# A linear-attention layer and its two-matrix MLP on one core: the four small products of an attention group are gathered into common stretches of TensorE, whose places follow a count of instructions

## Chip, core and metric

The kernel runs on one core of a Trainium2 chip. The time is that of one execution in microseconds on the device; lower is better. The kernel before was timed in three runs: 470.63, 470.05 and 470.16 us, median 470.16. One further execution was profiled, and all rows below are from it: its span, from the first to the last instruction, is 470.0 us.

## What is computed

For each of 4 batches and 8 heads a 48x48 state is carried over 768 steps: decayed by a gate, increased by an outer product, read by a query. The result, 3072 tokens of 384, goes through two matrices with a clipped square between them.

```python
    f = 1.0 / (1.0 + np.exp(-f_logit))
    for t in range(S):
        state = f[:, :, t, :, None] * state + np.einsum('bhd,bhe->bhde', k[:, :, t], v[:, :, t])
        y[:, :, t] = np.einsum('bhd,bhde->bhe', q[:, :, t], state)
...
    h = x @ w_in
    g = np.where(pos, h, np.where(neg, 0.0, (h + beta) ** 2 / (4.0 * beta)))
    return (g @ w_out).astype(np.float32)
```

## The kernel before

**The MLP.** Tokens are taken in 6 steps of 128 positions (4 batches, so 512 columns). A step has 16 units, one for each 128 of the 2048 hidden features: 96 units, numbered 0 to 95. `unit_1` computes a hidden block with 9 matmuls of 128x512 (`mm_in`, L265): inputs and weights are split into a high and a low part, and three of the four products are kept, for 3 slices of the input. ScalarE and VectorE then apply the activation and split it again (L268 to L282); `unit_2` adds its part of the output with 9 more matmuls (`mm_out`, L289). TensorE runs `unit_1` of unit u and then `unit_2` of unit u-1.

**The attention.** A step has 4 pairs of heads; two pairs form a group. The groups of steps 1 to 5 are named by their first pair: 4, 6, 8, ... 22. A group needs on TensorE: *scores* (`scores_of_two`, L657: keys times queries, masked afterwards on VectorE at L663), *states* (`states_by_parts`, L791, from keys that were transposed before: on TensorE, L676, for step 1, on VectorE, L690, from step 2 on), and *outputs* in three parts: `begin` and the last part (`attended`, L712: masked scores times values) and between them the products of queries and carried states (L739). The result is rounded into `x` (L695, L696), and part of it is moved between partitions by six DMAs (`moved`, line L307). All these are small float32 matmuls of 48 to 64 rows.

**The order.** `Plan` collects all operations with a cost from `COST`, deduces a start time for each, and the program is written in that order. TensorE's own order is that of the calls: at unit u after `unit_1(u)` come the visits that two tables list. `TURNS` gives for a pair the unit of its transposition, `VISITS` for a group the units of scores, of `begin` together with states, and of outputs. A run of small products between two large ones is called a *stretch* here. Where the plan sees TensorE idle for over 500 ns, it fills the gap with products of zeros (`warm`, L342).

**Loads.** Weights, keys and queries, gates and values come over SP's queue in the order of the plan.

Of the kernel before, what the change touches and what calls it, by code (L numbers as in the profile page):

```python
# [23 lines left out]
C = 128  # L24
# [25 lines left out]
SMALL_PRODUCTS = ("scores", "scores_half", "heads", "thirds", "both", "begin", "before", "part", "states", "parts", "turn")  # L50
# [3 lines left out]
COST = dict(mm=227, narrow=120, scores=1000, scores_half=500, heads=960, thirds=1020, both=1090, begin=480, before=930, part=560, states=850, parts=830, turn=350, first=110, last=95,  # L54
# [3 lines left out]

LOOK, MARGIN, GAP = ("ACT", "DVE"), 100, 3000

TURNS = {4: 6, 5: 6, 6: 9, 7: 9, 8: 16, 9: 16, 10: 23, 11: 23, 12: 28, 13: 28, 14: 35, 15: 35, 16: 43, 17: 43, 18: 53, 19: 53, 20: 58, 21: 58, 22: 69, 23: 69}
VISITS = {4: (6, 7, 8), 6: (9, 11, 12), 8: (16, 20, 23), 10: (23, 25, 28), 12: (28, 32, 35), 14: (35, 41, 43), 16: (43, 47, 53), 18: (53, 56, 58), 20: (58, 64, 69), 22: (69, 73, 74)}
# [3 lines left out]
AFTER = {0: (('turn', 0), ('turn', 1)), 1: (('states', 0),), 3: (('turn', 2), ('turn', 3)), 4: (('states', 2),)}  # L66

# [15 lines left out]
class Plan:  # L83
# [7 lines left out]
    def add(self, engine, cost, emit, *deps, kb=0, near=0):  # L91
# [24 lines left out]

    def order(self):
        index = {o: n for n, o in enumerate(self.ops)}
        for o in reversed(self.ops):
            tail = o.cost + (LANDING + PER_KB * o.kb + (ADDING if o.engine == "POOL" else 0) if o.kb else o.near)  # L120
            o.late = min((u.late - o.lag(u) for u in o.users), default=0) - tail - o.early
# [12 lines left out]
        while done < len(self.ops):  # L134
# [28 lines left out]
            o.start = t  # L163
            free[e] = t + o.cost
# [17 lines left out]
def gla_moe(ctx: ExitStack, tc: tile.TileContext, ff, kqd, f0, vv, vad, vbd, wd, fixedd, gates, values, headsd, out):  # L182
# [22 lines left out]
    state, ds = sd[:R, 0:NP * B * D].rearrange("r (g e) -> r g e", e=D), sd[:R, NP * B * D:]  # L205
# [4 lines left out]
    later = y3[:, 0, 0:2 * B * D].bitcast(F32)  # L210
# [10 lines left out]
    f0s = const.tile([128, NI * NT * B + 1], F32, name="f0s")  # L221
    half, up, down, top_of = (const.tile([128, 1], F32, name=a) for a in ("half", "up", "down", "top_of"))
# [105 lines left out]
    set_ds = add("POOL", 200, lambda: fresh(ds[:, 2 * B * D:]))  # L328
# [16 lines left out]
    add("PE", 4000, lambda: warm(12), set_zeros)  # L345
# [176 lines left out]
    def elementwise(n):  # L522
# [10 lines left out]
        elif i == 0:  # L533
            c["lv"] = dma(va if p == 0 else vb, vad if p == 0 else vbd, 512 if p == 0 else 768)
        else:
            c["lv"] = dma(v[k], vv[i, p // 2], 384, old(n - 4, "y", "st"), att[2]["st"], moved[1] if i > 1 else None)
# [12 lines left out]
        if i > 0:  # L549
# [3 lines left out]
            def decayed():  # L553
                for b in range(B):
                    nc.scalar.activation(ds[:, at + b * D:at + (b + 1) * D], state[:, p * B + b], AF.Copy, scale=whole(kq[p])[:R, b:b + 1])  # L555

            c["db"].append(sca(B * COST["decay"], decayed, d, state_of[i - 1, p // 2], old(n - 2, "y", "se"), set_ds))
# [80 lines left out]
    def borrowed(k):  # L638

        return [(6, ph[(k + 1) % 2].rearrange("p (b c) -> p b c", b=B), [gs[k - 1]["3"]]), bank(2)]  # L640
# [6 lines left out]
    def scores_of_two(n, k):  # L647
# [13 lines left out]
        c["am"] = d["am"] = []  # L661
        for h, (b, ps, _) in enumerate(held):
            o = vec("dve", lambda h=h, ps=ps: nc.vector.tensor_tensor(  # L663
                out=masked(n)[h], in0=by_block(ps), in1=mask_t.rearrange("u (o t) -> u o t", o=1).broadcast_to([C, 2 * B, T]), op=ALU.mult),
                c["sc"], ready["mask_t"], old(n - 4, "y"), att[2]["y"], att[2]["st"])
            c["am"].append(o)
        freed(k, held, *c["am"])
# [32 lines left out]
    def attended(n, other):  # L700
# [4 lines left out]
        def emit():  # L705
            for m in range(B):
                for e, k in TILES:
# [5 lines left out]
                                     masked(n)[h][half, block], start=other and m == 0, stop=not other and m == B - 1)  # L713
# [3 lines left out]
    def begin(n):  # L717
# [6 lines left out]
        c["yb"] = add("PE", "begin", attended(n, True), c["am"], c["lv"], d["lv"], [b[2] for b in held])  # L724

    def outputs(n):
# [5 lines left out]
        def emit():  # L732
            for k, before in ((1, later), (0, ds)):
                for m in range(B):
                    for e, h in TILES:
# [4 lines left out]
                                         start=False, stop=False)  # L740
# [6 lines left out]
        def third(t):  # L747
            return [moved.get(i - 1)] + c["se"] if t == NT else [free]
# [29 lines left out]
    def states_by_parts(n, k):  # L778
# [3 lines left out]
        held = borrowed(k)  # L782
        sums = [wide(b[1])[:R, 0:2 * B * D] for b in held]

        def emit():
            for e in range(2):
# [6 lines left out]
        c["st"] = d["st"] = add("PE", "parts", emit, c["kn"], d["kn"], c["lv"], d["lv"], [b[2] for b in held])  # L793
        s = state[:, p * B:(p + 2) * B].rearrange("r b e -> r (b e)")
        o = vec("sums", lambda: nc.vector.tensor_tensor(out=later, in0=sums[0], in1=ds[:, 0:2 * B * D], op=ALU.add),
                c["st"], c["db"], d["db"], old(n - 2, "y", "se"), moved.get(i - 1))
# [7 lines left out]
        freed(k, held, o, z)  # L804
# [196 lines left out]

    for n, u in TURNS.items():
        groups.setdefault(u, []).append((1, n))
    for n, at in VISITS.items():
        for kind, u in zip((2, 3, 0), at):
            groups.setdefault(u, []).append((kind, n))
    for u in range(len(order_of)):
# [3 lines left out]
        for kind, n in sorted(groups.get(u, [])):  # L1011
            if kind == 0:
                outputs(n)
            elif kind == 1:
# [5 lines left out]
            elif kind == 2:  # L1020
                scores_of_two(n, u)
            else:
                begin(n)
                states_by_parts(n, u)
# [13 lines left out]
    with tc.manual_schedule():  # L1038
        idle, loaded = 0, False
        for o in plan.order():  # L1040
# [3 lines left out]
            if o.engine == "PE":  # L1044
# [148 lines left out]
```

## Time and profile before

| | |
|---|---|
| median of 3 runs | 470.16 us (470.05 to 470.63) |
| span of the profiled execution | 470.0 us |
| TensorE busy (matmuls) | 464.1 us, 99% |
| VectorE busy | 368.7 us, 78% |
| ScalarE busy | 264.9 us, 56% |
| granted clock of TensorE | full in all 40 slices |
| DMA | 54.34 MB, mean 116 GB/s |

Busy time of TensorE is the union of pipelined matmuls, with modelled ends; a matmul's own duration (390 ns) is longer than its place in the stream. So the useful measure is the distance between the starts of two groups of matmuls.

### The profile page before, as it was taken

Reading aid. Unit: us, or ns where it says so; the run is one execution under the profiler, and the core shown is the slowest. Engines: PE = TensorE matmul, PEld = TensorE weight load, DVE = VectorE, ACT = ScalarE, POOL = GpSimd, SP = SyncE. Lnnn points to the kernel's source line nnn. Section 1 sums busy time; section 2 is a strip of 40 time slices with the busy share of each in tenths; the row PEclk is TensorE's granted clock in tenths of the full one; section 3 lists DMA queues with packets and bytes.
Section 4 is the critical chain, followed back from the end, with each engine's and each line's share of the span. In section 5 each row is a group of like instructions: output and inputs, shape, how many; then the busy total and the mean of one; then the engine's idle time right before and its main releaser. Section 6 shows DMA issues by size and latency. Waiting matters only on the chain.

```text
span 470.0 us, 10963 instructions
## 1 busy us (share of the span) xinstructions
PE 464.1 (99%) x4551; PEld 378.1 (80%) x4551; DVE 368.7 (78%) x704; ACT 264.9 (56%) x483; POOL 25.5 (5%) x67
## 2 busy tenths in 40 slices
PE   9999999999999999999999999999999999999996
PEld 4887888778888888888888888888888888888885
DVE  7989998998999988999889879665766565655553
ACT  4589888955464654645545465544455444544443
POOL 4100020020000001002000002000000000000000
PEclk9999999999999999999999999999999999999999
DMA  8788758363031241401133141133403233423211
GB/s 295 244 269 275 257 170 269 131 176 107 1 81 78 63 120 70 135 23 47 49 90 94 52 138 57 56 81 100 158 20 113 74 101 89 158 89 91 89 45 70
DMA packets 21331, 54.34 MB, mean 116 GB/s; under 512 B 3328, under 2 KB 5504, under 8 KB 21280
## 3 DMA queue, kind: packets, MB, share of 16 engines
q1 hardware_dynamic: 21184, 53.53, 36.3%
q8 instruction: 36, 0.59, 0.5%
q14 instruction: 15, 0.12, 0.1%
q10 hardware_dynamic: 96, 0.10, 0.1%
HBM read 44.76 MB, written 4.72 MB: 105 GB/s over the span
## 4 chain that ended last, share of the span: by engine, by line
PE 81%; DMA 9%; DVE 6%; ACT 2%; issue 1%; SPq 0%; ACTq 0%; DVEq 0%
PE po L289 38%; PE ph L265 37%; DMA raw<-in_w 8%; PE pa L739 2%; PE pa L712 2%; DVE bits L397 2%; DVE w_lo L402 1%; PE ph L657 1%; DMA kq<-in_kq 1%; ACT bits L395 1%; DVE x L696 1%; PE pa L791 1%; DVE glo L282 1%; PE ph L791 1%; DVE act L276 1%
## 5 line engine op out<-in xcount | busy, mean ns | idle before, releaser
L265 PE MATMUL ph<-x,w_hi 128*128 128x512 f32 x570 | 145.3, 390 | 0.4 <-ACT w_hi L401 0.3
L268 ACT ACTIVATE act<-ph,half 128x512 f32<-128x512 f32 x96 | 65.9, 687 | 116.2 <-PE ph L265 115.3
L265 PEld LDWEIGHTS ph<-x,w_hi 128*128 128x128 f32 x570 | 106.7, 188 | 23.6 <-ACT w_hi L401 0.7
L276 DVE SCALAR_TENSOR_TENSOR act<-ph,act 128x512 f32<-128x512 f32 x96 | 66.1, 688 | 53.2 <-ACT act L271 52.1
L279 ACT CAST ghi<-act 128x512 fp32r<-128x512 f32 x96 | 59.6, 620 | 58.4 <-DVE act L276 58.1
L289 PE MATMUL po<-ghi,w_hi 128*128 128x512 f32 x287 | 85.7, 400 | 0.1
L289 PE MATMUL po<-ghi,w_lo 128*128 128x512 f32 x287 | 82.8, 390 | 0.0
L289 PE MATMUL po<-glo,w_hi 128*128 128x512 f32 x287 | 82.6, 389 | 0.0
L282 DVE TENSOR_TENSOR glo<-act,ghi 128x512 fp32r<-128x512 f32 x96 | 66.1, 689 | 18.2 <-ACT ghi L279 16.3
L265 PE MATMUL ph<-x,w_lo 128*128 128x512 f32 x285 | 80.0, 389 | 0.0
L690 DVE STREAM_TRANSPOSE kn<-kq 32x128 f32<-32x128 f32 x224 | 67.8, 302 | 3.6
L289 PEld LDWEIGHTS po<-ghi,w_lo 128*128 128x128 f32 x287 | 53.9, 188 | 11.5
L289 PEld LDWEIGHTS po<-glo,w_hi 128*128 128x128 f32 x287 | 53.9, 188 | 11.5
L265 PEld LDWEIGHTS ph<-x,w_lo 128*128 128x128 f32 x285 | 53.5, 188 | 11.1
L271 ACT ACTIVATE act<-act 128x512 f32<-128x512 f32 x96 | 60.7, 632 | 2.8
L289 PEld LDWEIGHTS po<-ghi,w_hi 128*128 128x128 f32 x287 | 52.0, 188 | 11.6 <-ACT ghi L279 0.7
L414 DVE TENSOR_REDUCE ok<-raw 128x1 f32<-128x512 f32 x48 | 31.2, 679 | 6.2 <-DMA raw<-in_w 6.0
L491 POOL COPY end<-w 128x4 f32<-128x4 f32 (+1 forms) x20 | 8.4, 419 | 259.9 <-DVE w L487 259.6
L487 DVE TENSOR_TENSOR_SCAN w<-f,least_w 128x512 f32<-128x512 f32 (+1 forms) x18 | 20.8, 1158 | 2.2 <-ACT f L483 2.2
L395 ACT ACTIVATE bits<-raw,top_of 128x512 uint32<-128x512 fp8e4 (+1 forms) x25 | 18.4, 741 | 6.7 <-DMA raw<-in_w 6.7
L494 DVE TENSOR_TENSOR_SCAN f<-f,rec 128x512 f32<-128x512 f32 (+1 forms) x18 | 20.8, 1157 | 0.1
L555 ACT ACTIVATE sd<-sd,kq 112x48 f32<-112x48 f32 x80 | 19.5, 326 | 1.1 <-POOL kq L504 1.1
(120 smaller groups left out, 382.6 us busy)
## 6 DMA issues: line engine op xcount, KB each, us to landing
raw<-in_w SPq DMA_DIRECT2D x21, 511.6 KB, 4.7
kq<-in_kq SPq DMA_DIRECT2D x18, 512.0 KB, 4.9
raw<-in_w SPq DMA_DIRECT2D x18, 512.0 KB, 3.6
out_y<-raw SPq DMA_DIRECT2D x17, 256.0 KB, 2.1
f<-in_f SPq DMA_DIRECT2D x16, 256.5 KB, 3.0
v<-in_v SPq DMA_DIRECT2D x10, 384.0 KB, 4.8
raw<-in_w SPq DMA_DIRECT2D x12, 256.0 KB, 2.9
kq<-kq SPq DMA_DIRECT2D x30, 64.2 KB, 2.7
```

The lines of the kernel that those rows point to most:

```text
L265: nc.tensor.matmul(ps[:, to], w_in(w_hi if high else w_lo, j, kt), xt[:, kt, t, c], start=(n == 0), stop=(n == 8))
L268: nc.scalar.activation(a, ps, AF.Relu, bias=half, scale=0.5)
L271: nc.scalar.activation(a, a, AF.Square)
L276: nc.vector.scalar_tensor_tensor(out=a, in0=ps, scalar=1.0, in1=a, op0=ALU.max, op1=ALU.min)
L279: nc.scalar.copy(hi, a)
L282: nc.vector.tensor_tensor(out=lo, in0=a, in1=hi.bitcast(F32), op=ALU.subtract)
L289: nc.tensor.matmul(po[e][:, c], w_out(part, j, e), g[:, of], start=(j == 0 and n == 0 and c.start == 0), stop=(j == NJ - 1 and n == 2))
L395: m = sca(COST["bits"] * n // W, lambda: nc.scalar.activation(t, top, AF.Abs, bias=top_of, scale=2.0 ** 30), loaded, made[k - 4] if k >= 4 ...
L414: seen.append(vec("dve", lambda z=z, op=op: nc.vector.tensor_reduce(out=ok[:, 1 + NG + z + c:2 + NG + z + c], in_=words_of(raw[2])[1].bitc ...
L487: s1 = vec(COST["scan"] if count == 1 else 602, lambda bwd=bwd, u0=u0, u1=u1: nc.vector.tensor_tensor_scan(out=wide(w[:, u0:u1]), data0=bw ...
L494: s2 = vec(COST["scan"] if count == 1 else 602, lambda fwd=fwd, b0=b0, b1=b1: nc.vector.tensor_tensor_scan(out=fwd, data0=fwd, data1=wide( ...
L690: nc.vector.transpose(kn[n % 2][u:u + 32, ::-1, r:r + 32], src[:, :, u:u + 32])
```

## The change

The four products of a group get their own unit each: `VISITS` has four entries, for scores, states, `begin` and outputs, and entries of different groups fall on the same unit, so that their products form one stretch. `visit` writes them in the order begin, states (if the scores of the group were earlier), scores, outputs, states (if the scores are in the same visit). `TURNS` lists a group once, and both its pairs are transposed there.

Buffers: the decayed states get a second buffer (`ds` in turn), the sum of state and decay gets its own (`later`, before a part of `y3`), states take banks 0 and 1 of PSUM when no outputs are under way, and where scores and states share a visit, ScalarE copies one half of the scores out of PSUM before it is masked. After `begin`, ScalarE copies 8 values of its result (`seen_y`), and the outputs wait for that copy.

The plan gets a model of the loading of TensorE's instructions: `fetched` counts instructions, takes blocks of 256 of which the first ends at 185, and delays an operation if the block it enters was asked for less than 4300 ns ago. Zeros are now decided inside the plan (`zeros_for`) and count as instructions.  The scratch of dynamic DMA is cut to 4096.

```diff
+INSTRUCTIONS = dict(scores=32, scores_half=16, heads=32, thirds=32, both=128, begin=64, before=128, part=64, states=64, parts=128, parts_last=64, zeros=24, turn=8)
+BLOCK, FIRST_BLOCK, AHEAD, FETCH = 256, 185, 40, 4300
...
-VISITS = {4: (6, 7, 8), 6: (9, 11, 12), 8: (16, 20, 23), 10: (23, 25, 28), 12: (28, 32, 35), 14: (35, 41, 43), 16: (43, 47, 53), 18: (53, 56, 58), 20: (58, 64, 69), 22: (69, 73, 74)}
+TURNS = {4: 4, 6: 7, 8: 11, 10: 20, 12: 25, 14: 35, 16: 40, 18: 52, 20: 58, 22: 66}
+VISITS = {4: (5, 5, 8, 8), 6: (8, 10, 10, 13), 8: (20, 20, 22, 22), 10: (22, 25, 28, 28), 12: (28, 33, 33, 40), 14: (40, 40, 43, 43), 16: (43, 48, 55, 55), 18: (55, 56, 56, 61), 20: (61, 61, 73, 73), 22: (73, 74, 74, 77)}
...
+def zeros_for(o, idle):
+    gap = o.start - idle if idle else 0
...
+    return int(gap * 0.9 / 230) if gap > 500 else 0
...
         o = Op(engine, cost, emit, flat, kb, near)
+        if engine == "PE":
+            o.count = INSTRUCTIONS.get(kind) or 2 * max(1, round(cost / (COST["mm"] if cost % COST["mm"] == 0 else COST["narrow"])))
...
+    def fetched(self, o, zeros):
+
+        self.at += 2 * zeros
+        t, step, last = o.start, o.cost / o.count, self.at
+        end = self.at + o.count
+        marks = sorted([(b - AHEAD, 0, b) for b in self.blocks(last + AHEAD, end + AHEAD)] + [(b, 1, b) for b in self.blocks(last, end)])
+        for at, kind, b in marks:
+            t += (at - last) * step
+            last = at
+            if kind:
+                t = max(t, self.came.get(b, 0))
+            else:
+                self.came[b + BLOCK] = t + FETCH
+        self.at = end
+        return t + (end - last) * step - o.start
...
-            c["db"].append(sca(B * COST["decay"], decayed, d, state_of[i - 1, p // 2], old(n - 2, "y", "se"), set_ds))
+            c["db"].append(sca(B * COST["decay"], decayed, d, state_of[i - 1, p // 2], old(n - 4, "y", "se"), set_ds))
...
+            if h == 1 and copied:
+                need = sca("copy", lambda ps=ps: nc.scalar.copy(masked(n)[1], by_block(ps)), need, past)
+                source = masked(n)[1]
...
-        c["yb"] = add("PE", "begin", attended(n, True), c["am"], c["lv"], d["lv"], [b[2] for b in held])
+        o = add("PE", "begin", attended(n, True), c["am"], c["lv"], d["lv"], [b[2] for b in held])
+        c["yb"] = sca("small", lambda: nc.scalar.copy(seen_y.rearrange("u (b c) -> u b c", b=B), held[0][1][0:1, :, T - 1:T + 1]), o)
...
+    def visit(u):
+
+        new, made, begun, ended = ([n for n, at in VISITS.items() if at[k] == u] for k in range(4))
+        held = [n for n, at in VISITS.items() if at[2] <= u <= at[3]]
+        for n in begun:
+            begin(n)
+        for n in made:
+            if n not in new:
+                states_by_parts(n, u, False)
+        for n in new:
+            scores_of_two(n, u, n in made)
+        for n in ended:
+            outputs(n)
+        for n in new:
+            if n in made:
+                states_by_parts(n, u, not held)
```

Three places show what moves. **TensorE at unit 4**, early in the program: the last large products of `unit_1(4)`, the state products of step 0 (L770) and the first large product of `unit_2(3)`. Before:

```order
L265 MATMUL ph_110<-x_85,w_hi 128x512 x6
L265 MATMUL ph_110<-x_85,w_lo 128x512 x3
L770 MATMUL pa_107<-v,am_78 48x48 x8
L770 MATMUL pa_107<-v,am_79 48x48 x8
L289 MATMUL po_112<-ghi_89,w_hi 128x512
L289 MATMUL po_113<-ghi_89,w_hi 128x512
```

After, from the third product of zeros that stands behind the same state products (L818 here) to the same large product:

```order
L382 LDWEIGHTS zeros
L382 MATMUL po_117<-zeros 128x512
L723 MATMUL pa_110<-fixed,kq_68 128x112 x4
L382 LDWEIGHTS zeros
L382 MATMUL po_117<-zeros 128x512
L382 LDWEIGHTS zeros
L382 MATMUL po_117<-zeros 128x512
L382 LDWEIGHTS zeros
L382 MATMUL po_117<-zeros 128x512
L723 MATMUL pa_111<-fixed,kq_69 128x112 x4
L329 MATMUL po_115<-ghi_89,w_hi 128x512
```

The transpositions of pairs 4 and 5 (L723; `kq_68` and `kq_69` hold their keys) have come here from unit 6, and three products of zeros stand ahead of each.

**TensorE at units 35 to 41**, the middle of the program. Before, the outputs of group 12 (L712 is their end) are followed by the scores of group 14 (L657) at unit 35:

```order
L712 MATMUL pa_108<-am_77,v 48x64
L712 MATMUL pa_107<-am_76,v 48x64
L712 MATMUL pa_108<-am_77,v 48x64
L657 MATMUL ph_110<-kq_70 64x64
L657 MATMUL pa_109<-kq_70 64x64
L657 MATMUL ph_110<-kq_70 64x64
```

and the states of group 14 (L791) come at unit 41, behind its `begin`:

```order
L712 MATMUL pa_107<-am_78,v 48x64
L712 MATMUL pa_108<-am_79,v 48x64
L712 MATMUL pa_107<-am_78,v 48x64
L791 MATMUL pa_109<-v,kn_80 48x48
L791 MATMUL ph_110<-v,kn_80 48x48 x2
L791 MATMUL pa_109<-v,kn_80 48x48 x2
```

After, all stand at unit 40: the scores of group 14 (L697), the outputs of group 12 (L787, then L759) and the states of group 14 (L839). The first join:

```order
L697 MATMUL pa_112<-kq_71 64x64
L697 MATMUL ph_114<-kq_71 64x64
L697 MATMUL pa_112<-kq_71 64x64
L787 MATMUL pa_110<-kq_68,later 48x64
L787 MATMUL pa_111<-kq_69,later 48x64
L787 MATMUL pa_110<-kq_69,later 48x64
```

and the last:

```order
L759 MATMUL pa_111<-am_77,v 48x64
L759 MATMUL pa_110<-am_76,v 48x64
L759 MATMUL pa_111<-am_77,v 48x64
L839 MATMUL pa_112<-v,kn_80 48x48
L839 MATMUL ph_114<-v,kn_80 48x48 x2
L839 MATMUL pa_112<-v,kn_80 48x48 x2
L839 MATMUL ph_114<-v,kn_80 48x48 x2
```

No large product is left between the four; the stretch has 448 instructions where the longest before has 320.

**ScalarE at unit 22**: the activation of unit 21 ends and that of unit 22 begins.

```order
L311 ACTIVATE act_84<-act_84 128x512
L319 CAST ghi_89<-act_84 128x512
L308 ACTIVATE act_83<-ph_113,half 128x512
L772 COPY seen_y<-pa_110 1x8
L311 ACTIVATE act_83<-act_83 128x512
L595 ACTIVATE ds<-sd,kq_71 112x48 x4
L523 ACTIVATE f_67<-f_67 128x513
```

The copy `seen_y` stands between the two steps of the activation of unit 22 (L308 and L311); before nothing stood there.

## Rows read from the trace of the kernel before

**Rows 1.** The page: the span, the busy time of TensorE (PE matmuls, PEld weight loads), and the granted clock in 40 slices, in tenths.

```profile
span 470.0 us, 10963 instructions
PE 464.1 (99%) x4551; PEld 378.1 (80%) x4551; DVE 368.7 (78%) x704; ACT 264.9 (56%) x483; POOL 25.5 (5%) x67
PEclk9999999999999999999999999999999999999999
```

**Rows 2.** All that TensorE's matmuls waited for: us in total, times, longest us.

```profile
PE ph L342 <- DVE zeros L315: 1.1, 1, 1.1
PE ph L265 <- ACT w_hi L401: 0.3, 1, 0.3
```

**Rows 3.** The chain of work that ended last, around three stretches: start us, us, what. First scores alone, then outputs and scores joined, then outputs alone; large products stand on both sides.

```profile
103.42 2.04 PE ph L265 x9
106.55 2.27 PE po L289 x9
...
159.48 2.04 PE ph L265 x9
161.52 1.04 PE pa L739 x64
163.94 2.27 PE po L289 x9
...
372.32 2.04 PE ph L265 x9
374.36 1.04 PE pa L739 x64
375.85 2.27 PE po L289 x9
```

**Rows 4.** TensorE's products of the scores by form, from the list of lines: count, then busy us and mean ns of one. The ten groups share them.

```profile
L657 PE MATMUL pa<-kq 48*64 48x64 f32 x320 | 11.3, 219 | 0.0
L657 PE MATMUL ph<-kq 48*64 48x64 f32 x320 | 11.3, 219 | 0.0
```

**Rows 5.** TensorE in order of time at unit 4: start us, us, operation, count.

```profile
41.67 1.43 PE L265 MATMUL ph<-x,w_hi 128*128 128x512 f32 x5 [0.26 <-ACT w_hi L401]
...
43.72 0.93 PE L770 MATMUL pa<-v,am 128*48 128x48 f32 x32
44.57 0.96 PE L289 MATMUL po<-ghi,w_hi 128*128 128x512 f32 x3
```

**Rows 6.** VectorE in order of time: the second scan of pair 4's gates, and the keys (L497) and queries (L499) of pairs 4 and 5; the rows between are left out.

```profile
35.54 1.22 DVE L494 TENSOR_TENSOR_SCAN f<-f,rec 128x512 f32<-128x512 f32 x1
...
42.86 0.68 DVE L497 TENSOR_TENSOR kq<-kq,w 128x512 f32<-128x512 f32 x1
...
44.92 1.22 DVE L487 TENSOR_TENSOR_SCAN w<-f,least_w 128x512 f32<-128x512 f32 x1
46.05 0.67 DVE L276 SCALAR_TENSOR_TENSOR act<-ph,act 128x512 f32<-128x512 f32 x1
...
50.37 0.69 DVE L497 TENSOR_TENSOR kq<-kq,w 128x512 f32<-128x512 f32 x1
50.98 0.69 DVE L499 TENSOR_TENSOR kq<-kq,f 128x512 f32<-128x512 f32 x1
```

**Rows 7.** The page's DMA queues: packets, MB, share of the time of 16 engines.

```profile
q8 instruction: 36, 0.59, 0.5%
```

**Rows 8.** DMA queues in five short windows, one after the other: 349.0 to 351.0 us (no packet at all), 351.0 to 352.1, 354.5 to 356.0, and then, around another stretch, 278.7 to 283.3 and 283.3 to 284.5 us. Columns as in rows 7.

```profile
DMA packets 0, 0.00 MB, mean 0 GB/s; under 512 B 0, under 2 KB 0, under 8 KB 0
...
q8 instruction: 1, 0.02, 5.5%
...
q8 instruction: 1, 0.02, 4.5%
...
q1 hardware_dynamic: 406, 1.34, 83.4%
...
q8 instruction: 1, 0.02, 4.6%
```

**Rows 9.** TensorE in order of time at the stretch of unit 69 and behind it.

```profile
349.70 0.66 PE L739 MATMUL pa<-kq,y 48*48 48x64 f32 x32
...
350.63 0.63 PE L712 MATMUL pa<-am,v 64*48 64x64 f32 x32
...
352.12 0.96 PE L289 MATMUL po<-ghi,w_hi 128*128 128x512 f32 x3
...
353.61 0.85 PE L289 MATMUL po<-glo,w_hi 128*128 128x512 f32 x3
354.30 0.61 PE L265 MATMUL ph<-x,w_hi 128*128 128x512 f32 x2
```

**Rows 10.** ScalarE in order of time at the stretch of unit 53, which begins at 276.03 us.

```profile
276.14 0.69 ACT L268 ACTIVATE act<-ph,half 128x512 f32<-128x512 f32 x1 [1.35 <-PE ph L265]
276.86 0.63 ACT L271 ACTIVATE act<-act 128x512 f32<-128x512 f32 x1
```

**Rows 11.** SP's queue behind the outputs of group 22: start us, us, what; and the page's row on these moves (KB each, us from issue to landing).

```profile
378.48 1.78 SPq L307 DMA_DIRECT2D x<-y  x3
...
380.92 1.77 SPq L307 DMA_DIRECT2D x<-y  x3
...
x<-y SPq DMA_DIRECT2D x30, 64.0 KB, 2.5
```

More of the change, by code (lines that the diff above doesn't have):

```diff
@@ L66 @@
 AFTER = {0: (('turn', 0), ('turn', 1)), 1: (('states', 0),), 3: (('turn', 2), ('turn', 3)), 4: (('states', 2),)}
+def zeros_for(o, idle):
+    gap = o.start - idle if idle else 0
+    if o.start < 20000 and gap > 250:
+        return int(gap / (330 if o.start < 10000 else 230)) + 1
+    return int(gap * 0.9 / 230) if gap > 500 else 0
 class Op:
@@ L163, in order @@
             o.start = t
+            if e == "PE":
+                o.zeros = zeros_for(o, idle)
+                o.cost = self.fetched(o, o.zeros)
+                idle = t + o.cost
             free[e] = t + o.cost
@@ L343, in warm @@
                                  start=opened["start"], stop=opened["start"])
-    add("PE", 4000, lambda: warm(12), set_zeros)
+    add("PE", "zeros", lambda: warm(12), set_zeros)
     piece = []
@@ L535, in elementwise @@
         else:
-            c["lv"] = dma(v[k], vv[i, p // 2], 384, old(n - 4, "y", "st"), att[2]["st"], moved[1] if i > 1 else None)
+            c["lv"] = dma(v[k], vv[i, p // 2], 384, old(n - 4, "y", "st"), att[2]["st"], moved.get(1) if i > 1 else None)
         if p == NP - 1:
@@ L712, in emit @@
                     nc.tensor.matmul(held[h][1][64 * e:64 * e + D, m, T * (1 - k):][:, :T], v[pr // 2][half, b, pr % 2 * 2 + h],
-                                     masked(n)[h][half, block], start=other and m == 0, stop=not other and m == B - 1)
+                                     masked(n)[h][half, block], start=other and m == 0, stop=m == B - 1, skip_group_check=not other)
         return emit
@@ L732, in emit @@
         def emit():
-            for k, before in ((1, later), (0, ds)):
+            for k, before in ((1, later), (0, ds[n // 2 % 2])):
                 for m in range(B):
@@ L803, in states_by_parts @@
         c["se"] = d["se"] = [o, z]
-        freed(k, held, o, z)
+        if alone:
+            banks[0], banks[1] = [o], [z]
+        else:
+            freed(k, held, o, z)
     firsts = [bank(k) for k in (3, 2, 0)]
@@ L1003, in gla_moe @@
         groups.setdefault(u, []).append((1, n))
-    for n, at in VISITS.items():
-        for kind, u in zip((2, 3, 0), at):
-            groups.setdefault(u, []).append((kind, n))
+    for u in {u for at in VISITS.values() for u in at}:
+        groups.setdefault(u, []).append((0, 0))
+    def visit(u):
[13 more added lines that the diff above has]
+                states_by_parts(n, u, not held)
     for u in range(len(order_of)):
@@ L1012, in gla_moe @@
             if kind == 0:
-                outputs(n)
-            elif kind == 1:
+                visit(u)
+                continue
+            for n in (n, n + 1):
                 prepare(n)
@@ L1038, in gla_moe @@
     with tc.manual_schedule():
-        idle, loaded = 0, False
+        loaded = False
         for o in plan.order():
@@ L1043, in gla_moe @@
                 loaded = True
-            if o.engine == "PE":
-                gap = o.start - idle if idle else 0
-                if o.start < 20000 and gap > 250:
-                    warm(int(gap / (330 if o.start < 10000 else 230)) + 1)
-                elif gap > 500:
-                    warm(int(gap * 0.9 / 230))
-                idle = o.start + o.cost
+            if o.engine == "PE" and o.zeros:
+                warm(o.zeros)
             o.emit()
```

56 lines of the change are left out of this document (30 added, 26 removed).

## The prediction, written before the changed kernel ran

> **What bounds the kernel now.** [...] The chain of waits gives its pace: nine large products take 2.04 us, 0.227 us each, and it has no other engine in it between them [rows 3]. Whatever ScalarE, VectorE and the DMAs do matters only where TensorE comes to wait for it.
>
> **What a join is worth.** Read the chain from the start of the last large group ahead of a stretch to the start of the next large group, take off the 2.04 us of the former, and add the 0.23 us by which the group behind a stretch is longer (2.27 for 2.04). Scores alone: 106.55 - 103.42 - 2.04 + 0.23 = 1.32 us. Outputs alone: 375.85 - 372.32 - 2.04 + 0.23 = 1.72 us. Both in one stretch: 163.94 - 159.48 - 2.04 + 0.23 = 2.65 us [rows 3]. One stretch less is worth 1.32 + 1.72 - 2.65 = **0.39 us**. From the tables: `VISITS` before names 23 different units (6, 7, 8, 9, 11, 12, 16, 20, ... 74), after 18 (5, 8, 10, 13, 20, 22, 25, 28, 33, 40, 43, 48, 55, 56, 61, 73, 74, 77). Five fewer: **-1.95 us**. The products themselves are the same in number and form.
>
> **Transpositions and zeros at unit 4.** The transpositions of pairs 4 and 5 stand at unit 4, between the state products of step 0 and `unit_2(3)`, with three products of zeros ahead of each. Before, `unit_2(3)` begins at 44.57 us, right behind the states that begin at 43.72 us, and the 0.26 us wait of unit 4 is over by then [rows 5]. Lower bound of the loss: six zeros at the pace of a large product, 6 x 0.227 = 1.36 us (the transpositions themselves only move). Upper bound: the second transposition needs the keys of pair 5, which VectorE had ready only after 50.98 us [rows 6]. VectorE's new order brings them forward: from the scan at 35.54 us to them stand three scans of 1.13 us (44.92 to 46.05), eleven elementwise steps of about 0.6 us (50.37 to 50.98) and a reciprocal, some 10.1 us [rows 6]; they would be done at 35.54 + 10.1 + 0.6 = 46.2 us if VectorE never waits, at 47.0 us if it waits for its inputs as in that part of before (0.8 us). TensorE would reach `unit_2(3)` at 46.8 to 47.6 us, of which 0.8 us is the moved work: a loss of 1.4 to 2.2 us. I take **+1.6 us**. No earlier slack covers it, since TensorE's stream is already unbroken here.
>
> **Blocks of instructions.** TensorE's instructions come in 36 packets [rows 7]; 4551 matmuls and 4551 weight loads [rows 1] make 253 in each, which fits the change's own block of 256 (a visit's 32 scores run as 64 matmuls each with its load: 640 in ten groups [rows 4], 128 instructions as in `INSTRUCTIONS`). A packet takes 0.5% of 16 x 470 us / 36 = 1.04 us. The change places stretches by this count, so I counted the rows of the new order myself, waits on semaphores included, with block ends at 185 + 256n. A stretch runs at (2.65 - 0.39) us / 320 = 7.1 ns an instruction, a block of it in **1.8 us**. Wherever a stretch holds two block ends, the next block must be there within 1.8 us of the first end. By my count four stretches do: unit 28 (its instructions 33 and 289), 40 (45, 301), 55 (73, 329) and 61 (46, 302). None before does: the longest have 320, and where a block ends inside them the next end lies ahead or among large products.
>
> The plan believes that it avoids this, but its count drifts. A large product right behind a stretch has its cost raised by `first`: 681 + 160 = 841 is no multiple of 227, so its count is 2 x round(841 / 120) = 14 for 6 instructions. Eight too many per stretch, less one or two uncounted semaphore waits: about 56 too many at unit 40. For the plan the block ends there at -11 and 245.
>
> How long a block takes is seen at unit 69. By my count a block ends at the 85th instruction of that stretch, about 350.3 us (349.70 to 350.63 us are 128 instructions [rows 9]). There is no packet from 349.0 to 351.0 us, and one from 351.0 to 352.1 us that takes 5.5% of 16 x 1.1 us = 0.97 us [rows 8]: landed 1.75 us after the block's end. That is the lower price: no wait (1.75 for 1.8). The next block's first instruction there is the 21st behind the stretch, at 354.6 us, and the large products come without a gap [rows 9]: upper price 4.3 us, a wait of 2.5 us. A third price lies between: behind the stretch of unit 53 a block ends at about 281.5 us, while other transfers fill 83.4% of the DMA engines until 283.3 us, and the packet comes only in the window after that [rows 8], 0.88 us long, so landed at 284.2 us at the earliest: 2.7 to 2.9 us. I take 2.8 us, the row between the ends: a wait of 1.0 us in four places, **+4.0 us** (0 to 10).
>
> [...]
>
> **What I cost at nothing.** ScalarE gets ten copies of 8 values and four of a half of the scores (0.6 us each, as its other steps of this width [rows 10]); it is 56% busy. But the outputs now wait for the small copy. At unit 53 the first step of the activation begins 0.11 us after the stretch, and the second at 276.86 us, 0.83 us after it [rows 10]; the copy stands between the two. The outputs follow `begin` (the outputs' own last part has the same products: 1.72 - 0.39 less the 0.93 us from 349.70 to 350.63 us [rows 9], 0.40 us) and the scores (1.32 - 0.39 = 0.93 us), so 1.33 us after the stretch begins: a copy of some 0.3 us leaves about 0.2 us. Two of the moves of `x` get less room: the outputs of groups 18 and 22 are now three units ahead of their use. In before the last move is issued at 380.92 + 1.77 us and lands 2.5 us later, 385.2 us [rows 11]: 9.3 us behind the end of the stretch at 375.85 us [rows 3], where five groups of 2.04 us give 10.2 us. It should just hold, if SP's queue is not held up by a weight load ahead of the moves.
>
> **Sum.** -1.95 + 1.6 + 4.0 = +3.65 us. The profiled execution's 470.0 us stand 0.16 us below the median of 470.16: **473.8 us**.
>
> **Rivals.**
> [...]
> - *Faster.* No block is waited for, the zeros cost their 1.36 us alone, and the wait of 0.26 us at unit 4 goes because the weights' part comes no later while TensorE comes later: 470.16 - 1.95 + 1.36 - 0.26 - a few tenths of other gaps = 469.1 us. It decides from a loss of 1.0 us at unit 4 downwards. Against it: six zeros alone take longer.
> - *The small copy is late.* If one step of the activation (0.63 us) slips ahead of it, the outputs wait 0.4 us in the six stretches that hold `begin`, scores and outputs (8, 22, 28, 43, 55, 73): 469.8 + 2.4 = 472.2 us without block waits.
> - *A block takes the upper price*: 4 x 2.5 for 4 x 1.0: 479.8 us.
>
> **How the numbers follow.** Block waits of clearly more than nothing 0.55 (0.15 of it near the upper price), none 0.25, faster 0.10, the late copy 0.10. The likeliest gives 473.8 us. The range runs from the faster case, 469.0, to near the upper price, 479.5 us. About 0.2%, 0.9 us, is what a measurement can tell. Faster by more than that 0.12 (the faster case and the edge of the first rival), within it 0.25, slower 0.63.
>
> **What would show it.** Right: TensorE's busy row falls below its share, and the order of time shows gaps of about 1 us inside the stretches of units 28, 40, 55 and 61, with no releaser, each ending soon after a q8 packet; stretches without a second block end cost 0.39 us less per join; `unit_2(3)` begins 2.2 to 3 us later than 44.57 us. Wrong: dense stretches without gaps (then blocks are not waited for), a wait of the outputs on `seen_y`, or of unit 64 or 80 on `x`.

## The result, and the profile after

The changed kernel took **474.78 us** (median of 4 runs, 474.22 to 475.55) beside 470.18 us for the kernel before (4 runs): ratio 1.0099, 95% interval 1.0086 to 1.0112. It is slower by 4.6 us, 1% of the time. Predicted were 473.8 us, 469.0 to 479.5.

The page of the profiled execution, which took 475.15 us: span, busy time of the engines, TensorE's busy share and its granted clock in 40 slices.

```profile
span 473.4 us, 11001 instructions
PE 463.4 (98%) x4556; PEld 378.9 (80%) x4556; DVE 368.8 (78%) x704; ACT 267.7 (57%) x497; POOL 22.9 (5%) x67
PE   8999999999999999998999998989999999999996
PEclk9999999999999999999999999999999999999999
```

TensorE's busy time fell by 0.7 us against [rows 1] while the span grew by 3.4 us: its stream of products takes a little less, and time in which TensorE does nothing was added. Beside the first slice three fall to 8, those that begin at 213, 284 and 308 us. The granted clock is 9 tenths or more in every slice, so these are waits. The list of what TensorE's matmuls waited for (us in total, times, longest):

```profile
PE pa L759 <- issue: 3.7, 3, 1.3
PE ph L382 <- DVE zeros L355: 1.1, 1, 1.1
PE po L329 <- ACT ghi L319: 0.4, 1, 0.4
PE po L619 <- DVE kq L539: 0.2, 1, 0.2
PE ph L305 <- ACT w_hi L441: 0.2, 1, 0.2
```

In [rows 2] there were two waits, 1.4 us in all, so the time before was the length of TensorE's own stream. The first line is new: 3.7 us in three waits, on no engine and no transfer ("issue"); two short ones, for ScalarE (0.4 us) and for keys (0.2 us), are new too. No line names `seen_y` or `x`. TensorE in order of time around the three (start us, us, operation, count, idle time before):

```profile
215.61 0.63 PE L787 MATMUL pa<-kq,sd 48*48 48x64 f32 x32
216.06 0.51 PE L759 MATMUL pa<-am,v 64*48 64x64 f32 x23
217.76 0.33 PE L759 MATMUL pa<-am,v 64*48 64x64 f32 x9 [1.19 <-issue]
...
286.73 0.28 PE L759 MATMUL pa<-am,v 64*48 64x64 f32 x5
288.20 0.65 PE L759 MATMUL pa<-am,v 64*48 64x64 f32 x27 [1.20 <-issue]
...
316.92 0.52 PE L759 MATMUL pa<-am,v 64*48 64x64 f32 x24
318.77 0.33 PE L759 MATMUL pa<-am,v 64*48 64x64 f32 x8 [1.32 <-issue]
```

These are units 40, 55 and 61. Each gap cuts one run of 32 equal products in two, behind the 23rd, 5th and 24th. Count the stretch up to there, two instructions for each product: unit 40 has 64 scores, 64 products of the queries with the state and 23 more, 151 products, 302 instructions. Unit 55 has 165 products, 330 instructions; unit 61 has 152, 304. The prediction had the second block end at the 301st, 329th and 302nd instruction. So TensorE stops within two instructions of a block's end as counted from the program.

What comes before the gap is in the DMA queues, here from 215.3 to 216.4 us, just ahead of the first gap's end (packets, MB, share of 16 engines).

```profile
DMA packets 1, 0.02 MB, mean 15 GB/s; under 512 B 0, under 2 KB 0, under 8 KB 0
...
q8 instruction: 1, 0.02, 5.7%
```

One instruction packet, alone on the queues, 5.7% of 16 x 1.1 us = 1.0 us long. By the trace's times of the packets it had landed at 216.38 us, and no other instruction packet came before TensorE went on at 217.76 us. At the other two gaps a packet lands at 286.71 and 317.44 us, 1.50 and 1.33 us ahead of the product that goes on.

### The profile page after: what moved, and what is told of

It reads as the page before. It is cut to its first block, busy times and chain, and to the rows that moved or that the text cites. A ratio compares the mean times of both kernels' runs of the same rounds, so it can differ in the third digit from the quotient of the medians.

```text
span 473.4 us, 11001 instructions
## 1 busy us (share of the span) xinstructions
PE 463.4 (98%) x4556; PEld 378.9 (80%) x4556; DVE 368.8 (78%) x704; ACT 267.7 (57%) x497; POOL 22.9 (5%) x67
## 4 chain that ended last, share of the span: by engine, by line
PE 87%; DVE 6%; ACT 3%; DMA 2%; issue 2%; SPq 0%; DVEq 0%
PE po L329 40%; PE ph L305 38%; PE pa L759 2%; PE pa L787 2%; PE ph L697 1%; DMA raw<-in_w 1%; DVE w L527 1%; DMA f<-in_f 1%; PE pa L839 1%; DVE f L534 1%; PE ph L839 1%; DVE bits L437 1%; ACT bits L435 1%; DVE kq L539 1%; ACT w_hi L441 1%
## 5 line engine op out<-in xcount | busy, mean ns | idle before, releaser
L308 ACT ACTIVATE act<-ph,half 128x512 f32<-128x512 f32 x96 | 66.0, 688 | 119.2 <-PE ph L305 118.5
L311 ACT ACTIVATE act<-act 128x512 f32<-128x512 f32 x96 | 60.7, 632 | 2.7
L531 POOL COPY end<-w 128x4 f32<-128x4 f32 (+1 forms) x20 | 6.7, 333 | 293.9 <-DVE w L527 293.7
L759 PE MATMUL pa<-am,v 64*48 64x64 f32 x640 | 13.8, 219 | 3.7 <-issue 3.7
```

What stands on the lines that cost most here:

```text
L308: nc.scalar.activation(a, ps, AF.Relu, bias=half, scale=0.5)
L311: nc.scalar.activation(a, a, AF.Square)
L759: nc.tensor.matmul(held[h][1][64 * e:64 * e + D, m, T * (1 - k):][:, :T], v[pr // 2][half, b, pr % 2 * 2 + h], masked(n)[h][half, block], ...
```

## The experiments

In all of them `warm(12)`, the first work of TensorE, is the place where instructions are put in (in experiment 5 also a later `warm`), so that every instruction behind it moves by the same count. In experiments 1 to 6 nothing else changes; 7 to 10 change more, on top of experiment 1. Cutting one product of zeros of 512 columns into four of 128 adds three products with their loads, six instructions.

**1. Moving all block ends by 72 instructions.**

```
     def warm(count):
-        for _ in range(count):
-            if opened["bank"] is not None:
+        for n in range(count):
+            if count == 12 and n < 12:
+                for _ in range(4):
+                    nc.tensor.matmul(opened["bank"][:, 0:128], zeros, zeros[:, 0:128], start=True, stop=True)
+            elif opened["bank"] is not None:
```

> The changed kernel with its first 12 products of zeros each cut into four of a quarter of the columns: the same columns, 72 instructions more ahead of everything else, nothing else moved. Theory of the blocks: by my count no stretch then holds two block ends, so the three gaps of 1.40, 1.41 and 1.54 us at units 40, 55 and 61 vanish and the time falls by 4.3 us, from 474.8 to about 470.5 us. Rival, a wait on data (the small copy, a bank of PSUM, ScalarE or VectorE late there): the gaps stay at the same products and the time stays at 474.8 us.

Measured: 470.46 us (10 runs, 470.02 to 472.01) beside 470.43 us for before (19 runs): ratio 1.0009, interval 0.9997 to 1.0022. All that TensorE waited for here, and then the chain's large products around the stretch of unit 40, first in the changed kernel and then here (start us, us, what):

```profile
PE ph L383 <- DVE zeros L355: 1.1, 1, 1.1
PE ph L305 <- ACT w_hi L444: 0.5, 1, 0.5
```

```profile
212.21 2.04 PE ph L305 x9
...
218.85 2.28 PE po L329 x9
```

```profile
211.98 2.04 PE ph L305 x9
217.17 2.28 PE po L329 x9
```

The three waits are gone, with 72 instructions more to run. From the large group ahead to the one behind, unit 40 took 6.64 us and takes 5.19: 1.45 us less. The same reading of units 55 and 61 gives 6.40 against 4.91 us and 6.73 against 5.19: the three are worth 1.45 + 1.49 + 1.54 = **4.48 us**. The time fell by 474.78 - 470.46 = 4.3 us. Nearly all of the slowdown is these three waits.

**2. The same kernel, 30 instructions.**

```
-            if count == 12 and n < 12:
+            if count == 12 and n < 5:
```

From the changed kernel's trace I had fitted a rule by then: the next block can be used 3.5 us after TensorE passes a point 36 instructions ahead of a block's end (it passes these at 214.30, 284.69 and 315.16 us by my count, and goes on at 217.76, 288.20 and 318.77). This run asks the rule for one gap of the three.

> The changed kernel with 5 of the first 12 products of zeros cut into four: 30 more TensorE instructions ahead. By the blocks of 256 (next block usable 3.5 us after a point 36 instructions ahead of a block's end) exactly one stretch then holds two block ends too close together: unit 55, with a gap of 1.45 us, and the gaps of units 40 and 61 are gone. Time: 470.3 us of the versions without gaps plus 1.45: 471.8 us. Rival (anything put ahead removes all gaps, or none): 470.4 or 474.8 us.

Measured: 471.71 us (10 runs, 471.05 to 473.08), ratio 1.0030, interval 1.0018 to 1.0041. TensorE's only wait of that kind, its place, and the chain's large products around it:

```profile
PE pa L790 <- issue: 1.5, 1, 1.5
```

```profile
283.87 0.51 PE L790 MATMUL pa<-kq,sd 48*48 48x64 f32 x22
285.90 0.33 PE L790 MATMUL pa<-kq,sd 48*48 48x64 f32 x9 [1.51 <-issue]
```

```profile
280.04 2.04 PE ph L305 x9
...
286.72 2.26 PE po L329 x9
```

It is unit 55. The gap moved from the 330th instruction of the stretch to the 300th (behind 32 + 64 + 32 + 22 = 150 products), into another run of products: 30 earlier for 30 instructions put ahead. The waits of units 40 and 61 are gone. From group to group the stretch takes 6.68 us, 1.77 more than the 4.91 without a gap, where the rule had 1.45.

**3. The remainder, not the amount.** The twelve products of zeros are cut into fifteen of 32 columns each: 336 = 256 + 80 instructions.

```
-                for _ in range(4):
-                    nc.tensor.matmul(opened["bank"][:, 0:128], zeros, zeros[:, 0:128], start=True, stop=True)
+                for _ in range(15):
+                    nc.tensor.matmul(opened["bank"][:, 0:32], zeros, zeros[:, 0:32], start=True, stop=True)
```

> The changed kernel with its first 12 products of zeros cut into fifteen of 32 columns each: 336 more TensorE instructions ahead, 256 + 80. Theory of blocks of 256: what counts is the number modulo 256, 80 lies between 52 and 92 where no stretch of this kernel holds two block ends, so the time is that of the version with +72, 470.5 us, with no gaps in the trace. Rival (the gaps depend on how much stands ahead, not on its remainder): +196 gave 489.4 us, so more than that, or 475 us at the least.

Measured: 470.04 us (10 runs, 469.33 to 470.93), ratio 0.9998, interval 0.9987 to 1.0009, no wait on "issue". So the remainder counts, and blocks of 256 fit. The traces say the same in another way: in the order of their starts, a multiple of 256 and 193 or 194 more of the instructions that a trace records of TensorE, semaphore waits included, stand ahead of the first product behind a gap, in all fourteen gaps of the four kernels that have any (the changed one and experiments 2, 4 and 5). In the changed kernel they are 4801, 6337 and 7105: 18, 24 and 27 times 256, and 193.

**4. Giving the order before the same fault.** The edit of experiment 1 in the kernel before, with seven products of zeros cut into four: 42 instructions.

```
-            if count == 12 and n < 12:
+            if count == 12 and n < 7:
```

> The kernel before, with its first 7 products of zeros each cut into four: 42 instructions more ahead of everything else. Theory of the blocks: by my count two block ends then fall into the stretches of units 53 and 69, which have 320 instructions: two gaps of about 1.4 us, 470.2 + 2.9 = 473.1 us. Rival (the gaps come from the new order of the products or the new buffers): no gap, 470.2 us.

Measured: 474.36 us (4 runs, 473.89 to 475.18), ratio 1.0082, interval 1.0064 to 1.0100: the order before, which had no wait, is as slow as the changed one. The waits; the chain's large products around units 53 and 69; and a window behind unit 69 (start:end, us, busy us of PE, PEld, DVE, ACT and POOL, granted clock, DMA share, GB/s):

```profile
PE pa L660 <- issue: 2.9, 2, 1.7
```

```profile
272.34 2.04 PE ph L265 x9
...
278.40 2.28 PE po L289 x9
...
347.62 2.04 PE ph L265 x9
...
353.96 3.44 PE po L289 x9
```

```profile
355.00:356.00 1.00, 1.00 (x4) 0.74 (x3) 1.00 (x3) 0.00 (x0) 0.00 (x0) 0.50 0.06 16
```

The two gaps stand at units 53 and 69, where the rule puts them. Their 2.9 us are the idle time in the list, as expected; but from group to group the two stretches take 6.06 and 6.34 us where the same joined stretch takes 4.46 [rows 3], so they cost 1.60 + 1.88 = 3.5 us. That is what two of the four runs show, 473.9 us with a mean clock of 1.000: 3.5 us above before. The profiled execution, 475.18 us, lost more through the clock: TensorE stood still for 1.7 us at unit 69, and from about 355 us on it was granted 0.50 (0.88 in the microsecond before, 0.92 from 358 to 359 us); the nine large products behind the stretch took 3.44 us for 2.28 behind that of unit 53.

**5. Many waits.** Fourteen products of zeros of the changed kernel are cut into eight: 196 instructions.

```
-            if count == 12 and n < 12:
-                for _ in range(4):
-                    nc.tensor.matmul(opened["bank"][:, 0:128], zeros, zeros[:, 0:128], start=True, stop=True)
+            if (count == 12 or count == 14 and n < 2):
+                for _ in range(8):
+                    nc.tensor.matmul(opened["bank"][:, 0:64], zeros, zeros[:, 0:64], start=True, stop=True)
```

> The changed kernel with the first 14 products of zeros each cut into eight: 196 instructions more ahead of everything else, the same columns. Theory of the blocks: by my count two block ends fall into the stretches of units 8, 22, 28, 40, 43, 61 and 73, and one more just behind that of unit 55; with 1.4 us for each of the seven and 0.5 us for the last the sum of gaps is 10.3 us instead of 4.35, so about 480.7 us, with gaps at units where none stands now (22, 43, 73). Rival, a wait on data: unchanged, 474.8 us.

Measured: 489.38 us (4 runs, 485.85 to 491.65), ratio 1.0399: the places came out, the time of about 480.7 us did not. All that TensorE waited for on "issue", and its longest other wait:

```profile
PE pa L790 <- issue: 5.7, 4, 2.1
PE po L329 <- ACT ghi L319: 2.4, 1, 2.4
PE ph L842 <- issue: 2.0, 2, 1.1
PE po L329 <- issue: 1.2, 1, 1.2
...
PE pa L762 <- issue: 1.1, 1, 1.1
```

Eight gaps stand at the eight stretches that the expectation names (units 8, 22, 28, 40, 43, 55, 61, 73), of 1.07 to 2.36 us from the start of the product ahead to that of the product behind: 11.7 us in all, without the products' own pace, for 10.3 expected. The expectation left out the wait for ScalarE, and the clock behind it:

```profile
66.00:67.00 1.00, 1.00 (x4) 0.77 (x3) 1.00 (x3) 1.00 (x4) 0.00 (x0) 0.50 0.82 319
```

At unit 7 TensorE waits 2.4 us for ScalarE, which itself waited 1.96 us there for a late part of the weights. This wait stands ahead of all eight gaps, so none of them brought it; why the weights came late the run doesn't show. Behind it, and again behind the 2.36 us gap of unit 8, the granted clock falls to 0.50 for 3 to 4 us, which loses 1.7 us each time (from the windows of one us). That is 11.7 + 2.4 + 3.4 = 17.5 us of the 19.0.

**6. The same edit where it should do nothing.** The kernel before with 72 instructions ahead.

```
-            if count == 12 and n < 7:
+            if count == 12 and n < 12:
```

> The kernel before with its first 12 products of zeros cut into four narrower ones each: 72 more TensorE instructions ahead of everything else, no other edit. Theory (blocks of 256, the next one usable 3.5 us after the sequencer passes a point 36 instructions ahead of a block's end): with +42 two dense stretches of this kernel held two block ends, with +72 none does, so its time is that of before, 470.2 to 470.6 us, and no gap stands in TensorE's trace. Rival (any instructions put ahead cost time of their own, by their number): it lies above the +42 version's 474.4 us. The run also gives a second trace of the order before, whose profiled execution had a span of 470.0 us where its timed runs have spans of 468.0 to 469.7 us: if that one execution was simply long, this span is about 468.5 us.

Measured: 471.31 us (10 runs, 469.83 to 472.99) beside 470.57 us (29 runs): ratio 1.0016, interval 1.0001 to 1.0030; span 469.5 us; no wait on "issue". The gaps of +42 are gone, 3 us with them. The 0.7 us that it lies above before barely clears its interval; two waits for keys, of 0.5 and 0.2 us, stand in its list that [rows 2] does not have. The second part of the expectation was a miss: this span is 469.5 us and not 468.5.

**7. The zeros of unit 4.** Experiment 1, and no products of zeros after the first 40 us.

```
-            if o.engine == "PE" and o.zeros:
+            if o.engine == "PE" and o.zeros and o.start < 40000:
```

> As e1_after_72, and without the six products of zeros at unit 4. If the zeros alone cost the 1.3 us by which the stretch of unit 4 is longer than its parts, this is 1.3 us faster than e1_after_72, about 469.2 us. Rival, the keys of pairs 4 and 5 are late and the zeros only fill the wait: the same time as e1_after_72, with a wait of TensorE on VectorE or ScalarE in their place.

Measured: 470.37 us (10 runs, 469.72 to 471.86), ratio 0.9999, interval 0.9986 to 1.0012: 0.1 us less for 1.3 expected. TensorE at unit 4, in the changed kernel and here:

```profile
42.98 0.93 PE L818 MATMUL pa<-v,am 128*48 128x48 f32 x32
43.84 0.82 PE L382 MATMUL po<-zeros 128*128 128x512 bf16 x3
44.49 0.59 PE L723 MATMUL pa<-fixed,kq 112*128 112x112 f32 x4
44.92 0.81 PE L382 MATMUL po<-zeros 128*128 128x512 bf16 x3
45.57 0.55 PE L723 MATMUL pa<-fixed,kq 112*128 112x112 f32 x4
45.89 0.94 PE L329 MATMUL po<-ghi,w_hi 128*128 128x512 f32 x3
```

```profile
43.79 0.93 PE L821 MATMUL pa<-v,am 128*48 128x48 f32 x32
45.30 0.60 PE L726 MATMUL pa<-fixed,kq 112*128 112x112 f32 x4 [0.58 <-ACT sd L825]
46.12 0.60 PE L726 MATMUL pa<-fixed,kq 112*128 112x112 f32 x4 [0.22 <-DVE kq L540]
46.49 0.95 PE L329 MATMUL po<-ghi,w_hi 128*128 128x512 f32 x3
```

Each three zeros take 0.65 us (43.84 to 44.49). Without them the transpositions wait for ScalarE's copy of the states out of their PSUM bank (0.58 us) and for the keys (0.22 us), and `unit_2(3)` begins 46.49 - 43.79 = 2.70 us behind the states, for 2.91 with the zeros. The zeros nearly only fill a wait; they don't make one.

**8 and 9. Transpositions one unit later.** Two edits of the tables on top of experiment 7; the second has one stretch less.

```
-TURNS = {4: 4, 6: 7, ...
-VISITS = {4: (5, 5, 8, 8), ...
+TURNS = {4: 5, 6: 7, ...
+VISITS = {4: (6, 6, 8, 8), ...     (second: 4: (7, 7, 8, 8))
```

> The changed kernel with +72 instructions ahead, and with the transpositions of pairs 4 and 5 at unit 5 instead of 4, their scores and state products at unit 6 instead of 5, and no products of zeros after the first 40 us. No stretch holds two block ends. At unit 4 the version with +72 spends 3.10 us on states, six zeros and transpositions; without the zeros it still spent 2.90 us, 1.27 of it waiting for ScalarE's copy of the states out of the same PSUM bank and for the keys. Theory (these waits exist only because the transpositions stand right behind the states): states alone 1.06 and transpositions alone 0.80 us, so 1.24 us less than the +72 version: 469.2 us, below before's 470.4. Rival (the keys of pair 5 or the ScalarE copies come no earlier, and the outputs at unit 8 then wait): within 0.3 us of the +72 version, 470.2 to 470.8 us.

Measured: 470.46 us (12 runs, 469.92 to 471.22), ratio 0.9999, interval 0.9989 to 1.0010. The rival holds in its time, not in its place: the wait reappears as one for ScalarE, not at unit 8 but still at unit 4.

```profile
43.50 0.93 PE L821 MATMUL pa<-v,am 128*48 128x48 f32 x32
45.19 0.97 PE L329 MATMUL po<-ghi,w_hi 128*128 128x512 f32 x3 [0.77 <-ACT ghi L319]
```

> As the version with the transpositions at unit 5, but with the scores and states of pairs 4 and 5 at unit 7, in one stretch with the transpositions of pairs 6 and 7: one stretch less, worth 0.39 us. Theory: 468.8 us. Rival (masks and sums between the scores and states at unit 7 and the outputs at unit 8 take longer than the group of 2.04 us between them, so the outputs wait 0.5 to 1 us): 469.3 to 470 us, with a gap of TensorE ahead of or inside the stretch of unit 8.

Measured: 472.78 us (6 runs, 471.63 to 474.23), ratio 1.0057, interval 1.0040 to 1.0074: worse than either theory. The wait is not ahead of the outputs, as the rival had it, but inside the stretch of unit 7:

```profile
61.40 0.60 PE L726 MATMUL pa<-fixed,kq 112*128 112x112 f32 x4 [0.98 <-DVE later L846]
62.56 0.57 PE L726 MATMUL pa<-fixed,kq 112*128 112x112 f32 x4 [0.56 <-DMA kq<-kq]
```

The transpositions of pairs 6 and 7 now stand behind the state products and wait until VectorE has read these out of the bank, and then for the keys: 1.5 us. The profiled execution is the shortest of the six, 471.63 us; where the other 1.15 us of the median went, its trace doesn't show.

**10. The early groups as before, the later ones as changed.** Also on top of experiment 7.

```
-TURNS = {4: 4, 6: 7, ...
-VISITS = {4: (5, 5, 8, 8), 6: (8, 10, 10, 13), ...
+TURNS = {4: 6, 6: 9, ...
+VISITS = {4: (6, 7, 7, 8), 6: (9, 11, 11, 12), ...
-        for kind, n in sorted(groups.get(u, [])):
+        for kind, n in sorted(groups.get(u, []), reverse=u < 10):
```

> The changed kernel with +72 instructions ahead, with pairs 4 to 7 at the units where the kernel before has them (transpositions at 6 and 9, ahead of the scores; scores, states and first outputs, outputs at 6, 7, 8 and 9, 11, 12), and no products of zeros after the first 40 us; the later groups as in the change. No stretch holds two block ends. Theory (two parts of the trace add up: from unit 4 to unit 20 the order before took 78.45 us in its +72 version, 1.53 us of it the scores of pair 8 at unit 16, which now stand at unit 20; from unit 20 to the end the changed order takes 347.2 us in its versions without gaps): 76.9 + 347.2 = 424.1 us from unit 4 on, where the versions without gaps have 424.6 to 425.7 and before 425.4 to 426.3. That is 1.2 us less than before: 469.3 us, ratio 0.997. Rival (VectorE and ScalarE set the pace up to unit 13 whatever TensorE's order there is, as two tries to take work off unit 4 suggest): no faster than the +72 version, 470.2 to 470.7 us.

Measured: 470.76 us (12 runs, 469.16 to 472.83), ratio 1.0012, interval 0.9996 to 1.0027. The rival holds again. From the states of unit 4 to the stretch of unit 20 it took 78.2 us (43.21 to 121.41), where 76.9 was expected and the +72 version needs 78.0: what was taken out of TensorE's order came back in small pieces. Set beside the trace of experiment 6 group by group, it takes 0.24 us more at unit 4 (0.17 of it a wait for ScalarE), 0.22 in the large products behind unit 6, 0.31 at unit 11 and 0.22 in those at unit 16: 1.0 of the 1.3 us. No version in these runs is faster than the kernel before beyond its interval.

## Why the prediction was right, step by step

**What a join is worth: right, but hidden.** The trace from unit 4 to its end compares the two orders without what precedes it, which differs by up to 1.3 us between the traces. State products of unit 4 in the order before with +72 (span 469.5 us), and in the changed order with +336 (span 467.6 us):

```profile
44.11 0.93 PE L773 MATMUL pa<-v,am 128*48 128x48 f32 x32
```

```profile
42.78 0.93 PE L821 MATMUL pa<-v,am 128*48 128x48 f32 x32
```

469.5 - 44.11 = 425.4 us against 467.6 - 42.78 = 424.8: 0.6 us shorter, where the joins' -1.95 and the 1.3 us at unit 4 make -0.65. But that is one pair of traces: with before's own trace (426.3 us) and that of +72 in the changed order (425.1 us) the difference lies anywhere from 0.3 to 1.5 us. The stretches alone say more. Read as the prediction reads three of them, all stretches behind unit 4 add up to 44.7 us (+72) and 45.1 us (before) in the order before, in 23 stretches, and to 42.1 us (+336) and 42.5 us (+72) in the changed order, in 19: 2.6 us less, with 2.2 and 3.0 as the extreme pairs. Of this 0.8 us are the transpositions of pairs 4 and 5, which went to unit 4: the scores of unit 6 took 2.10 us with them, scores alone take 1.32. So the joins are worth about 1.8 us (1.4 to 2.2) for the 1.95 forecast. The count was not quite right: there are four stretches fewer and not five, since the transpositions of pairs 6 and 7, which `VISITS` does not list, now stand alone at unit 7. The chain's row of them in +336:

```profile
60.23 0.77 PE pa L726 x8
```

In the times of whole executions the gain is lost: 1.0009 and 0.9998 for the two versions without gaps.

**Transpositions and zeros at unit 4: the size just under its lower bound, the cause wrong.** `unit_2(3)` begins 45.89 - 42.98 = 2.91 us behind the states, before 44.57 - 43.72 = 0.85 us [rows 5]: 2.06 us, of which 0.8 us only moved, so a loss of 1.3 us for the +1.6 taken. The keys were no upper bound (the second transposition didn't wait). But six zeros were not the price: experiment 7 leaves them out and gains 0.1 us, with waits for ScalarE's copy and for the keys in their place.

**Blocks of instructions: the mechanism right, two of its sizes off and nearly cancelling.** Predicted were four waits of 1.0 us, +4.0; there are three of 1.45 to 1.54 us, +4.5. That a price too low by a third and a count too high by one met so closely is luck; that there would be waits, their cause and three of the four places were forecast.

- *The price.* A block's landing was read well: the three packets land 1.84, 1.74 and 1.99 us behind the first block end by my count, and the row at unit 69 had said 1.75. What failed was to take the landing for the moment of use. TensorE goes on 1.33 to 1.50 us after it, 3.2 to 3.3 us behind the block end; the stretch had 1.8 us of work, so 1.4 us are lost. The "third price" of 2.8 us was chosen by delayed packets; no delay is needed. Delays do occur: in experiment 5, with block ends counted in its trace, the packets at units 8 and 55 begin 1.9 and 1.8 us behind the first end, where the other six begin 0.6 to 0.9 us behind theirs, and TensorE goes on 4.2 and 4.1 us behind that end, close to the upper price of 4.3.
- *The places.* Unit 28 holds two block ends and doesn't wait. Its first end is its 33rd instruction, the others' the 45th, 73rd and 46th. Its packet begins at 160.21 us, 0.6 us ahead of the block's end, and the others 0.7 to 0.8 us behind theirs; it landed at 161.33 us, 1.30 us before it was needed. If a request goes out some 36 to 46 instructions ahead of an end, as I fitted it, it falls there among the large products ahead of the stretch, at 0.11 us an instruction, so it comes 1 us early. That is argued from the positions; the run with +30 agrees: it has unit 55's first end at the 43rd instruction and waits, units 40 and 61 at the 15th and 16th and they don't.
- *How many blocks are held.* Blocks of 256 hold (experiments 1 to 3). The three waits say that TensorE doesn't have the block behind a stretch's second end when it comes to the first: its packet lands 1.74 to 1.99 us later. How many blocks TensorE holds at a time, no run shows.

**What I cost at nothing: right for the outputs and the moves, not quite for ScalarE.** No wait on `seen_y` and none on `x` stands in the list, and the late copy falls with that. One wait for ScalarE is new, 0.4 us ahead of the large products behind unit 7, and the chain of work that leads to it runs through one of the new copies of half the scores (L707):

```profile
59.52 0.47 ACT am L707
...
61.03 0.53 ACT ghi L319
```

The lists of experiments 1 and 3 don't have this wait. With no block waited for, the sum without its 4.0 us, the time would be 469.8 us; the versions without gaps took 470.0 to 470.5 us.

**Sum.** The sum set the span of 470.0 us beside the median of 470.16 as though both were the same thing. Every run's time is 1.75 to 1.93 us above its span (475.15 and 473.4), so the profiled execution of before had taken about 471.8 us, 1.6 more than the median. The forecast was worked from the median, so nothing hung on it. The profiled execution of after also closes: from unit 4 it takes 473.4 - 42.98 = 430.4 us, 5.6 more than the 424.8 of the +336 version, of which 4.5 are the three gaps, 0.65 the transpositions of unit 7 with their wait for ScalarE, and 0.4 a pause inside the stretch of unit 8. The versions without gaps lose between nothing and 0.4 us at these two places.

**What stays open.** Whether VectorE, ScalarE or the arrival of the weights sets the pace up to unit 13: four orders of TensorE's work there (experiments 1, 7, 8 and 10) gave one time within 0.1%, a fifth (9) was slower, and no run changed these engines' work. Open is also why the order before with +72 lies 0.7 us above before, and when a block is asked for: the 36 instructions are a fit.

## What to carry to other kernels

Where a stretch of short instructions runs faster than its instructions are brought (here 1.8 us for a block of 256 that could be used 3.2 to 3.3 us behind the end before it), count the program's instructions: in these runs a stretch that holds two block ends, the first of them not close behind its beginning, cost a wait of 1.1 to 2.4 us that names no engine, and the same stretch a few dozen instructions further along cost nothing. Between 30 and 336 TensorE instructions put ahead moved these waits, took them away or brought them, also into a kernel that showed none before (experiment 4). So where a change alters how many stand ahead, test for this by putting cheap instructions at the start before believing that an order is better or worse. Products of zeros in a place where other engines are late were worth next to nothing here when they were taken out (0.1 us for six).

## What the runs showed of the hardware that I had not expected

- Landing is not use. In 13 of 14 gaps of this kind, in four kernels, TensorE goes on 1.18 to 1.50 us behind the end of an instruction packet, in the other 1.62 us.
- A wait can cost more than it lasts. The waits of 1.19 to 1.32 us in the changed kernel were followed by a clock of 1.00, but those of 1.7 us (unit 69 of before with +42) and of 2.15 and 2.4 us idle (units 8 and 7 of the changed kernel with +196) by 3 to 4 us at 0.50 or near it, which lost 1.7 us each. It need not follow: two other runs of before with +42 have a mean clock of 1.000.
- Put far ahead of a gap, 30 instructions moved it by 30 instructions, and with 336 there was no gap, as with 72.
